# K as one tile of 64 KB rows in an attention decode kernel, with both products first and wo loaded near the end

## The chip, the cores and the metric

One core of a Trainium2 chip. The time is the device time of one execution in us. The experiments e1 to e4, e7, e10 and e11 ran on one chip and e5, e6, e8 and e9 on another, each beside the kernel before on the same chip (medians of 658.7 to 658.9 on both). A ratio below is the mean time of one kernel's fast runs over that of the other's of the same rounds, with a 95% interval; it is not quite the ratio of the medians that stand beside it.

## The reference, cut to what matters

One decode step for two rows: layernorm, attention over a cache of 8192 positions with 32 heads of 128, output projection, a second layernorm and a small ReLU-gated FFN.

```python
q = (layernorm(x) @ wq)                                  # 2 x 32 heads x 128
scores = einsum("bhqd,bhkd->bhqk", q, k_cache) / sqrt(128)
o = einsum("bhqk,bhkd->bhqd", softmax(scores), v_cache)  # k_cache, v_cache: 2 x 32 x 8192 x 128 bf16
h = x + o @ wo
h2 = h + ffn(layernorm(h))
```

The two caches are 268 of the 281 MB that are read, each byte used once.

## The kernel before

The work is cut into 16 passes of 4 heads. A pass has 8.4 MB of K and 8.4 MB of V. K comes in two halves of 4.2 MB into two buffers (rows of 32 KB), V in one tile (rows of 64 KB) into one buffer. For each half of K, DVE multiplies 96 of 128 positions of a row with q and folds the products by additions; TensorE transposes the other 32 and multiplies them with q; ACT takes the exps. When both halves have their exps, TensorE multiplies them with V (64 matmuls).

```python
K = [sb(f"K{i}", [128, SLOT], BF16) for i in range(2)]     # 32 KB a row each
V = sb("V", [128, 2 * SLOT], BF16)                         # 64 KB a row
...
# DVE, loop over passes
for q in range(PG):                                        # the two halves
    if q == 0:
        nc.vector.wait_ge(g2d, 1)
    nc.vector.wait_ge(k_sem[q], 16)
    nc.vector.sem_inc(k2p, 1)                              # TensorE may start
    run_d(k_mult(q))                                       # product
    last_d()
    nc.vector.sem_inc(d2s, 1)                              # K half free (for DVE)
    k_adds(q, run_d, last_d)                               # four folding additions
    if q == 0:
        nc.vector.wait_ge(p2d, 1)
        normalize(Ob, run_d, last_d)
        ...
    run_d(k_reduce(q))
    last_d()
    nc.vector.sem_inc(d2a, 1)                              # ACT: exps of DVE's part
...
# SP, pass by pass (p counts halves)
if p + 2 < NP:
    sp.wait((d2s, p + 1), tokp("kf", p))                   # product done, transposes done
    load_k(p + 2)
if p % 2 == 1 and p < P0 - 3:
    sp.wait(tokp("pv", p))                                 # all 64 products with V done
    load_v(p // 2 + 1, 0, 2 * J, v_sem[0])
```

The softmax here doesn't subtract the row's maximum and nothing guards it: scores larger than these inputs give would overflow.

## Time and profile before

| | |
|---|---|
| time before, beside the changed kernel | 659.11 us median of 6 (658.75 to 659.39) |
| one period (a K pair and a V tile, 16.78 MB) | 38.77 us |
| DVE busy in it | 28.80 us |
| V's load issued ahead of the leading DMA engine's turn | 10.3 to 11.9 us in the steady periods |

The timeline of the kernel before, SyncE's issues alone (start, length, line, what is loaded; the first line merges two issues, of K's first half at 312.34 and of its second at 327.75):

```profile
312.34 15.74 SPq L186 DMA_DIRECT2D K<-in_A_k_cache_dram  x2
341.20 0.33 SPq L189 DMA_DIRECT2D V<-in_A_v_cache_dram  x1
```

(The single transfer records don't name the engine. In the stream 16 packets are under way at a time, and nearly all start within 6 ns of the end of another; by that I put them in 16 rows below, and every tile then has 8 of its 128 packets in each row, in the order of issue.)

### The profile page before, as it was taken

The page shows a single profiled execution, that of the slowest core. Times are in us where ns is not written, and L with a number is a line of the kernel's source. Part 1 is how long each engine was busy: PE and PEld are TensorE (multiplying, and loading weights), DVE is VectorE, ACT ScalarE, POOL GpSimd, SP SyncE. Part 2 cuts the span into 40 slices and gives each one's busy share as a digit, 9 for nine tenths or more (in the row PEclk, how much of TensorE's full clock was granted, in tenths as well). Part 3 has the DMA queues.
Part 4 walks back from the last instruction along what each step waited for, and adds up shares of the span by engine and source line. Part 5 has one row for each costly group of instructions (what it writes and reads, how often), then busy time and mean ns, then how long its engine had stood idle before and what let it go on. Part 6 is the DMA issues. An engine that isn't in the chain of part 4 may idle for free.

```text
span 657.5 us, 7820 instructions
## 1 busy us (share of the span) xinstructions
PE 306.7 (47%) x3096; PEld 202.9 (31%) x3097; DVE 469.1 (71%) x275; ACT 274.0 (42%) x687; POOL 25.5 (4%) x96
## 2 busy tenths in 40 slices
PE   2644345444354445436444443644445354445466
PEld 0331232323233232323314232331323233133234
DVE  1594594958949496794949769494985949589881
ACT  1642343433454254344424534442454435335271
POOL 4000000000000000000000000000000000002000
PEclk9856557655575755557565575756557575556676
DMA  9999999999999999999999999999999999999997
GB/s 383 422 437 430 437 439 419 470 391 447 425 462 433 403 447 415 470 397 439 445 419 458 403 447 417 443 441 423 443 419 462 405 437 447 417 429 433 429 421 310
DMA packets 8629, 281.17 MB, mean 428 GB/s; under 512 B 966, under 2 KB 1068, under 8 KB 1580
## 3 DMA queue, kind: packets, MB, share of 16 engines
q1 hardware_dynamic: 8612, 281.06, 99.3%
q8 instruction: 5, 0.08, 0.1%
q14 instruction: 4, 0.03, 0.0%
q10 hardware_dynamic: 8, 0.00, 0.0%
HBM read 281.05 MB, written 0.00 MB: 427 GB/s over the span
## 4 chain that ended last, share of the span: by engine, by line
DMA 80%; DVE 15%; PE 3%; issue 1%; ACT 0%; DVEq 0%; SPq 0%
DMA K<-in_A_k_cache_dram 69%; DVE prod L563 15%; DMA V<-in_A_v_cache_dram 5%; DMA K<-in_B_W_gate_dram 4%; DMA V<-in_A_wq_dram 2%; PE T L345 1%; PE O L428 1%; PE O L272 1%; ACT kT L589 0%; PE O L775 0%; PE O L827 0%; PE O L330 0%; PE Ob L440 0%; PE T L405 0%; DVE prod L281 0%
## 5 line engine op out<-in xcount | busy, mean ns | idle before, releaser
L563 DVE TENSOR_TENSOR prod<-K,q_c 128x12288 bf16<-128x12288 bf16 x32 | 209.9, 6558 | 146.7 <-DMA K<-in_A_k_cache_dram 136.0
L572 DVE TENSOR_TENSOR prod<-prod 128x6144 bf16<-128x6144 bf16 (+3 forms) x128 | 212.2, 1658 | 7.8
L405 PE MATMUL T<-ident_f,K 128*128 128x128 f32 x512 | 123.3, 403 | 134.6 <-DVEq L611 134.6
L589 ACT ACTIVATE kT<-T 128x1024 bf16<-128x1024 bf16 x128 | 127.1, 1022 | 122.7 <-PE T L405 118.7
L428 PE MATMUL O<-V,e 128*16 128x512 bf16 x1024 | 91.4, 533 | 111.8 <-DMA V<-in_A_v_cache_dram 111.8
L517 ACT ACTIVATE e<-scores 32x96 bf16<-32x96 f32 x128 | 53.9, 421 | 196.5 <-DVEq L625 193.3
L405 PEld LDWEIGHTS T<-ident_f,K 128*128 128x128 f32 x512 | 88.6, 206 | 137.6 <-DVEq L611 137.5
L428 PEld LDWEIGHTS O<-V,e 128*16 128x16 bf16 x1024 | 30.5, 117 | 165.3 <-DMA V<-in_A_v_cache_dram 113.3
L388 PE MATMUL S<-q_c,kT 128*128 128x8 bf16 x1024 | 48.6, 171 | 44.8 <-ACT kT L589 44.6
L388 PEld LDWEIGHTS S<-q_c,kT 128*128 128x128 bf16 x1024 | 41.9, 107 | 73.1 <-ACT kT L589 71.3
L440 PE MATMUL Ob<-sel,os_sb 128*128 128x4 f32 x136 | 30.2, 345 | 38.4 <-ACT os_sb L592 38.4
L440 PEld LDWEIGHTS Ob<-sel,os_sb 128*128 128x128 f32 x136 | 28.7, 312 | 40.3 <-ACT os_sb L592 40.2
L517 ACT ACTIVATE e<-S 32x32 bf16<-32x32 f32 x128 | 29.8, 233 | 16.1 <-PE S L388 15.0
L577 DVE TENSOR_REDUCE scores<-prod 128x96 f32<-128x768 bf16 x32 | 30.5, 953 | 2.8
L517 ACT ACTIVATION_READ_ACCUMULATOR e<-scores 32x1 f32 x128 | 30.0, 235 | 0.0
L517 ACT ACTIVATION_READ_ACCUMULATOR e<-S 32x1 f32 x128 | 25.6, 200 | 1.5
L589 ACT ACT_TABLE_LOAD x15 | 19.2, 1283 | 0.3
L560 POOL COPY q_c<-q_all 128x144 bf16<-128x144 bf16 x16 | 7.5, 472 | 243.5 <-PE O L428 231.3
L592 ACT ACTIVATE os_sb<-O 128x512 f32<-128x512 f32 x17 | 10.1, 597 | 15.3 <-PE O L428 14.9
L544 POOL MEMSET O_l<- 128x32 bf16 x13 | 1.7, 130 | 299.8 <-DVEq L622 299.8
L281 DVE CAST prod<-O 128x512 bf16<-128x512 f32 x1 | 0.7, 692 | 11.0 <-PE O L272 11.0
L272 PE MATMUL O<-V,xlT 128*2 128x512 bf16 x32 | 3.4, 600 | 7.7 <-DMA V<-in_A_wq_dram 7.7
(103 smaller groups left out, 94.2 us busy)
## 6 DMA issues: line engine op xcount, KB each, us to landing
K<-in_A_k_cache_dram SPq DMA_DIRECT2D x32, 4096.0 KB, 29.2
V<-in_A_v_cache_dram SPq DMA_DIRECT2D x3, 4096.0 KB, 31.7
V<-in_A_wq_dram SPq DMA_DIRECT2D x1, 4096.0 KB, 12.3
X<-in_A_wo_dram SPq DMA_DIRECT2D x1, 3584.0 KB, 46.2
V<-in_A_v_cache_dram SPq DMA_DIRECT2D x1, 3072.0 KB, 23.1
K<-in_B_W_up_dram SPq DMA_DIRECT2D x1, 1376.0 KB, 23.6
K<-in_B_W_gate_dram SPq DMA_DIRECT2D x1, 1376.0 KB, 26.6
V<-in_A_v_cache_dram SPq DMA_DIRECT2D x1, 1024.0 KB, 25.2
```

Source lines behind the costliest of these rows:

```text
L272: mm = nc.tensor.matmul(Op[i][32 * t:32 * t + B, :], lhsT=lT[:, c * B:(c + 1) * B], rhs=wq[:, c, n:n + 512], start=(c == 0), stop=(c == DC ...
L388: i = nc.tensor.matmul(Sp[p % 2][:, A * jj:A * jj + 2 * A], lhsT=kv_[:, k, r, :], rhs=q_c[:, 2 * A * r:2 * A * r + 2 * A], start=(r == 0), ...
L405: i = nc.tensor.transpose(Tp[g % 2][:, k * 128:(k + 1) * 128], k_t[:, j:j + 2, :].rearrange("p j d -> p (j d)").bitcast(F32), ident_f[:])
L428: i = nc.tensor.matmul(Op[0][c:c + 16, :], lhsT=e_t[q][:, j // VJ, :], rhs=v_t[:, j:j + VJ, :].rearrange("p j d -> p (j d)"), start=(q == ...
L440: i = nc.tensor.matmul(Ob[:, 0:A], lhsT=os_sb[:, jj * Dh:(jj + 1) * Dh], rhs=sel[:, A * jj:A * jj + A], start=(jj == 0), stop=(jj == VJ - 1))
L517: i = nc.scalar.activation(out=e_t[q][h, j0 // VJ:j1 // VJ, :].rearrange("p g (j a) -> p g j a", a=A)[:, :, :, a], in_=src(h, a), func=ACT ...
L560: nc.gpsimd.tensor_copy(out=q_c[:], in_=q_all[:, o]).then_inc(g2d, 1)
L563: return nc.vector.tensor_tensor(out=prod[:, 0:JC, :], in0=tile(K[p % 2], p)[:, 0:JC, :], in1=q_c[:, Q2:QW].unsqueeze(1).broadcast_to([128 ...
L572: run(nc.vector.tensor_tensor(out=prod[:, 0:JC, 0:w], in0=prod[:, 0:JC, 0:w], in1=prod[:, 0:JC, w:2 * w], op=ALU.add))
L577: return nc.vector.tensor_reduce(out=scores[p % PG][:, 0:JC], in_=prod[:, 0:JC, 0:8], axis=AX.X, op=ALU.add)
L589: to_pe(nc.scalar.activation(out=kT[gg % 2][:], in_=Tp[gg % 2][:].bitcast(BF16), func=ACT.Copy))
L592: to_pe(nc.scalar.activation(out=os_sb[:], in_=Op[0][:], func=ACT.Copy))
```

## The change

Intent: K gets the packets of 64 KB that V has. The room for it: K becomes one buffer of 64 KB rows, so the next K can only load once both halves of this one have been read. Hence DVE makes both products first, into two scratch tiles (wo's tile X serves as the second, so wo loads near the end), and TensorE takes both halves in a row, with the sums and exps on ACT behind.

```diff
-        K = [sb(f"K{i}", [128, SLOT], BF16) for i in range(2)]
+        K = sb("K", [128, 2 * SLOT], BF16)
+        prods = [X[:, 0:JC * Dh].rearrange("p (j d) -> p j d", d=Dh), prod]
 ... TensorE, loop
                     k_part(body, 0, (1, 2, 3, 4), ((k2p, 1),))
-                    collect(body, 6)
-                    k_part(body, 1, (8, 9, 10, 11), ((k2p, 2),))
-                    pv(body, 0, ((JC, J, ((v_sem[0], 16),)), (0, JC, ())))
-                    pv(body, 1, ((JC, J, ((v_sem[1], 16), (a2p, 12))), (0, JC, ((a2p, EV),))))
+                    k_part(body, 1, (5, 6, 7, 8), ())
+                    collect(body, 9)
+                    pv(body, 0, ((JC, J, ((v_sem, 16), (a2p, 10))), (0, JC, ((a2p, 12),))))
+                    pv(body, 1, ((JC, J, ()), (0, JC, ((a2p, EV),))))
 ... DVE, loop
-                    for q in range(PG):
-                        ... wait, k_mult(q), k_adds(q), (normalize), k_reduce(q)
+                    for q in range(PG):
+                        run_d(k_mult(q, prods[q]))
+                    last_d()
+                    nc.vector.sem_inc(d2s, 1)
+                    for q in range(PG):
+                        k_adds(prods[q], run_d, last_d)
+                        if q == 0:
+                            nc.vector.wait_ge(p2d, 1)
+                        run_d(k_reduce(q, prods[q]))
+                        last_d()
+                        nc.vector.sem_inc(d2a, 1)
+                        if q == 0:
+                            nc.vector.sem_inc(d2s, 1)
+                            normalize(Ob, run_d, last_d)
 ... ACT, loop: all 8 evictions, then sums(), both exp_pe, both exp_dve
 ... SP
-                    if p + 2 < NP:
-                        sp.wait((d2s, p + 1), tokp("kf", p))
-                        load_k(p + 2)
+                    if p % 2 == 1 and p < P1:
+                        o = p // 2 + 1
+                        sp.wait((d2s, 2 * o - 1), tokp("kf", p))
+                        if o < NI:
+                            load(K, A_k_cache, o, k_sem[0])
+                            sp.wait(tokp("pv", p))
+                            load(V, A_v_cache, o, v_sem)
+                        else:
+                            ... half of K, wo into X, the other half, V in three pieces
```

More of the change, by code (lines that the diff above doesn't have):

```diff
@@ L95, in bass_sequential_preLN__gqa_block_cached__glu_gated_reglu__decode_kernel @@
         k_sem = [S(f"k{i}") for i in range(2)]
-        v_sem = [S(f"v{i}") for i in range(2)]
+        v_sem = S("v")
         a2p, k2p, l2p = S("a2p"), S("k2p"), S("l2p")
@@ L167, in bass_sequential_preLN__gqa_block_cached__glu_gated_reglu__decode_kernel, with kv_rows, load @@
         ZC = 64
-        def k_rows(p):
-            hq, b = divmod(p // 2, B)
-            return A_k_cache[b, A * hq:A * hq + A].rearrange(
-                "h (p k j) d -> k (h p) (j d)", p=128 // A, k=2)[p % 2]
-        def v_rows(o):
+        def kv_rows(cache, o):
             hq, b = divmod(o, B)
-            return A_v_cache[b, A * hq:A * hq + A].rearrange("h (p j) d -> (h p) (j d)", p=128 // A)
+            return cache[b, A * hq:A * hq + A].rearrange("h (p j) d -> (h p) (j d)", p=128 // A)
         def tile(x, p):
-            return x[:].rearrange("p (k j d) -> p k j d", j=J, d=Dh)[:, p % 2 if x is V else 0]
+            return x[:].rearrange("p (k j d) -> p k j d", j=J, d=Dh)[:, p % 2]
         if True:
             def program():
-                def load_k(p):
-                    nc.sync.dma_start(K[p % 2][:], k_rows(p)).then_inc(k_sem[p % 2], 16)
-                def load_v(o, k0, k1, sem):
-                    nc.sync.dma_start(V[:, k0 * Dh:k1 * Dh], v_rows(o)[:, k0 * Dh:k1 * Dh]).then_inc(sem, 16)
+                def load(x, cache, o, sem, k0=0, k1=2 * J):
+                    nc.sync.dma_start(
+                        x[:, k0 * Dh:k1 * Dh], kv_rows(cache, o)[:, k0 * Dh:k1 * Dh]).then_inc(sem, 16)
                 nc.scalar.dma_start(x_row, A_x[:, 0]).then_inc(sem_x, 16)
@@ L194, in program @@
                     wo_rows, A_wo[128 * DR:].rearrange("(p r) n -> p (r n)", r=4)).then_inc(sem_wl, 16)
-                load_k(0)
-                load_k(1)
+                load(K, A_k_cache, 0, k_sem[0])
                 pool.run(nc.gpsimd.memset(ident_f[:], 0.0))
@@ L317, in program @@
                 sp.wait(t_q)
-                load_v(0, 0, 2 * J, v_sem[0])
-                nc.sync.dma_start(
-                    X[:], A_wo[0:128 * DR].rearrange("(p r) n -> p (r n)", r=DR)).then_inc(sem_wo, 16)
+                load(V, A_v_cache, 0, v_sem)
                 t_mm, t_cp = {}, {}
@@ L361, in program @@
                                  start=True, stop=True)
-                nc.tensor.sem_inc(v_sem[1], 16 * (NI - 1))
                 EV = 13
@@ L373, in mark @@
                         self.at[key] = pe.run(inst)[1] - self.base
-                body = Tokens(pe.count)
+                body, tail = Tokens(pe.count), Tokens(0)
                 def k_part(T, p, ev, k_wait):
-                    k_t = tile(K[p % 2], p)
+                    k_t = tile(K, p)
                     wait = nc.tensor.wait_ge
@@ L390, in score @@
                                     rhs=q_c[:, 2 * A * r:2 * A * r + 2 * A], start=(r == 0), stop=(r == 1))
-                                if loop and g == NG - 2 and k == r == 0:
+                                if loop and p % 2 and g == NG - 2 and k == r == 0:
                                     T.mark(("kf", p), i)
@@ L434, in pv @@
                             n += 1
-                    T.mark(("pv", p), i)
+                    if T is tail or q:
+                        T.mark(("pv", p), i)
                 def collect(T, a):
@@ L469, in program @@
                     nc.tensor.sem_inc(l2p, -1)
-                    for sem in v_sem:
-                        nc.tensor.sem_inc(sem, -16)
-                    nc.tensor.sem_inc(k2p, -2)
+                    nc.tensor.sem_inc(v_sem, -16)
+                    nc.tensor.sem_inc(k2p, -1)
                     nc.tensor.sem_inc(a2p, -EV)
@@ L475, in program @@
                 pe.count = body.base + NI * n_body
-                tail = Tokens(0)
                 P0, P1 = NP - 2, NP - 1
@@ L489, in program @@
                 tail.mark("op", i)
-                pv(tail, P0, ((JC, J, ((v_sem[0], 16),)), (0, JC, ((a2p, 13),))))
+                pv(tail, P0, ((JC, J, ((v_sem, 16),)), (0, JC, ((a2p, 13),))))
                 nc.tensor.wait_ge(a2p, 14)
@@ L558, in q_copy, with k_mult, k_adds @@
                     else:
-                        pool.wait(tokp("fp", 2 * o - 2), (d2s, 2 * o))
+                        pool.wait(tokp("fp", 2 * o - 2), (d2s, 2 * o - 1))
                     nc.gpsimd.tensor_copy(out=q_c[:], in_=q_all[:, o]).then_inc(g2d, 1)
-                def k_mult(p):
+                def k_mult(p, pr):
                     return nc.vector.tensor_tensor(
-                        out=prod[:, 0:JC, :], in0=tile(K[p % 2], p)[:, 0:JC, :],
+                        out=pr[:, 0:JC, :], in0=tile(K, p)[:, 0:JC, :],
                         in1=q_c[:, Q2:QW].unsqueeze(1).broadcast_to([128, JC, Dh]), op=ALU.mult)
-                def k_adds(p, run, last):
+                def k_adds(pr, run, last):
                     w = Dh
@@ L572, in k_adds, with k_reduce @@
                         run(nc.vector.tensor_tensor(
-                            out=prod[:, 0:JC, 0:w], in0=prod[:, 0:JC, 0:w], in1=prod[:, 0:JC, w:2 * w], op=ALU.add))
+                            out=pr[:, 0:JC, 0:w], in0=pr[:, 0:JC, 0:w], in1=pr[:, 0:JC, w:2 * w], op=ALU.add))
                     last()
-                def k_reduce(p):
+                def k_reduce(p, pr):
                     return nc.vector.tensor_reduce(
-                        out=scores[p % PG][:, 0:JC], in_=prod[:, 0:JC, 0:8], axis=AX.X, op=ALU.add)
+                        out=scores[p % PG][:, 0:JC], in_=pr[:, 0:JC, 0:8], axis=AX.X, op=ALU.add)
                 def exp_pe(p):
@@ L605, in last_d @@
                             nc.vector.wait_ge(d2d, n_d[0])
+                    nc.vector.wait_ge(g2d, 1)
+                    nc.vector.wait_ge(k_sem[0], 16)
+                    nc.vector.sem_inc(k2p, 1)
                     for q in range(PG):
-                        if q == 0:
-                            nc.vector.wait_ge(g2d, 1)
-                        nc.vector.wait_ge(k_sem[q], 16)
-                        nc.vector.sem_inc(k2p, 1)
-                        last_d()
-                        run_d(k_mult(q))
-                        last_d()
-                        nc.vector.sem_inc(d2s, 1)
-                        k_adds(q, run_d, last_d)
+                        run_d(k_mult(q, prods[q]))
[3 more added lines that the diff above has]
+                        k_adds(prods[q], run_d, last_d)
                         if q == 0:
                             nc.vector.wait_ge(p2d, 1)
+                        run_d(k_reduce(q, prods[q]))
[3 more added lines that the diff above has]
+                            nc.vector.sem_inc(d2s, 1)
                             normalize(Ob, run_d, last_d)
@@ L622, in program @@
                             nc.vector.sem_inc(d2g, 1)
-                        run_d(k_reduce(q))
-                        last_d()
-                        nc.vector.sem_inc(d2a, 1)
-                    for sem, n in ((d2d, n_d[0]), (g2d, 1), (p2d, 1), (k_sem[0], 16), (k_sem[1], 16)):
+                    for sem, n in ((d2d, n_d[0]), (g2d, 1), (p2d, 1), (k_sem[0], 16)):
                         nc.vector.sem_inc(sem, -n)
@@ L630, in program @@
                 with nc.Fori(0, NI, engines=OrderedEngineSet([nc.scalar.engine])):
-                    n_a = 0
+                    n_a = (NG + 1) * PG
                     for q in range(PG):
                         for gg in range(NG):
-                            n_a += 1
-                            nc.scalar.wait_ge(p2a, n_a)
+                            nc.scalar.wait_ge(p2a, (NG + 1) * q + gg + 1)
                             evac(gg)
-                        n_a += 1
-                        nc.scalar.wait_ge(p2a, n_a)
+                    nc.scalar.wait_ge(p2a, n_a)
+                    sums()
+                    for q in range(PG):
                         exp_pe(q)
-                        if q == 0:
-                            sums()
+                    for q in range(PG):
                         nc.scalar.wait_ge(d2a, q + 1)
@@ L660, in program @@
                         dve.last()
-                        t_dm[p] = dve.run(k_mult(p))
-                        k_adds(p, dve.run, dve.last)
+                        t_dm[p] = dve.run(k_mult(p, prod))
+                        k_adds(prod, dve.run, dve.last)
                         if p == P0:
-                            dve.wait(tokp("pv", p - 2))
-                        t_s[p] = dve.run(k_reduce(p))
+                            dve.wait(tokp("pv", p - 1))
+                        t_s[p] = dve.run(k_reduce(p, prod))
                         if p == P0:
@@ L697, in program @@
                         exp_dve(p)
-                    if p + 2 < NP:
-                        sp.wait((d2s, p + 1), tokp("kf", p))
-                        load_k(p + 2)
-                    if p % 2 == 1 and p < P0 - 3:
-                        sp.wait(tokp("pv", p))
-                        load_v(p // 2 + 1, 0, 2 * J, v_sem[0])
-                    elif p == P0 - 3:
-                        sp.wait(tokp("pv", p))
-                        load_v(NI - 1, 0, J, v_sem[0])
-                    elif p == P0 - 2:
-                        load_v(NI - 1, J, 2 * J, v_sem[1])
-                    elif p == P0 - 1:
-                        sp.wait(tokp("pv", p - 1))
-                        load_v(NI, 0, J, v_sem[0])
-                        sp.wait(tokp("pv", p))
-                        for k, (j0, j1) in enumerate(((V_LAST, J), (0, V_LAST))):
-                            load_v(NI, J + j0, J + j1, sem_vl[k])
+                    if p % 2 == 1 and p < P1:
[6 more added lines that the diff above has]
+                        else:
+                            load(K, A_k_cache, o, k_sem[0], 0, J)
+                            sp.wait((d2s, 2 * o))
+                            nc.sync.dma_start(
+                                X[:], A_wo[0:128 * DR].rearrange("(p r) n -> p (r n)", r=DR)).then_inc(sem_wo, 16)
+                            load(K, A_k_cache, o, k_sem[1], J, 2 * J)
+                            sp.wait(tokp("pv", p))
+                            load(V, A_v_cache, o, v_sem, 0, J)
+                            for k, (j0, j1) in enumerate(((V_LAST, J), (0, V_LAST))):
+                                load(V, A_v_cache, o, sem_vl[k], J + j0, J + j1)
                     if p == NP - 2:
@@ L719, in program @@
                             nc.sync.dma_start(
-                                K[0][:, k * DC * F:(k + 1) * DC * F],
+                                K[:, k * DC * F:(k + 1) * DC * F],
                                 w.rearrange("(p c) n -> p (c n)", c=DC)).then_inc(sem_w[k], 16)
@@ L723, in program @@
                             nc.sync.dma_start(
-                                K[0][:, 2 * DC * F + r0 * D:2 * DC * F + (r0 + n) * D],
+                                K[:, 2 * DC * F + r0 * D:2 * DC * F + (r0 + n) * D],
                                 B_W_down[r0 * 128:(r0 + n) * 128].rearrange("(p r) n -> p (r n)", r=n)).then_inc(sem_wd[k], 16)
@@ L758, in program @@
                     in1=Sp[0][:, 0:B].unsqueeze(1).broadcast_to([128, DC, B]), op=ALU.subtract))
-                wup, wgt = (K[0][:, k * DC * F:(k + 1) * DC * F].rearrange("p (c f) -> p c f", c=DC)
+                wup, wgt = (K[:, k * DC * F:(k + 1) * DC * F].rearrange("p (c f) -> p c f", c=DC)
                             for k in range(2))
-                wdn = K[0][:, 2 * DC * F:2 * DC * F + 10 * D].rearrange("p (r n) -> p r n", n=D)
+                wdn = K[:, 2 * DC * F:2 * DC * F + 10 * D].rearrange("p (r n) -> p r n", n=D)
                 pe.wait(t_d)
```

## The prediction

> **What bounds the kernel now.** I began with the page of the kernel before: its slices, its queues, its chain.
>
> ```profile
> DVE  1594594958949496794949769494985949589881
> ...
> DMA  9999999999999999999999999999999999999997
> ...
> DMA packets 8629, 281.17 MB, mean 428 GB/s; under 512 B 966, under 2 KB 1068, under 8 KB 1580
> ...
> q1 hardware_dynamic: 8612, 281.06, 99.3%
> ...
> DMA 80%; DVE 15%; PE 3%; issue 1%; ACT 0%; DVEq 0%; SPq 0%
> ```
>
> See that the DMA row is at 9 in every slice but the last, and that one queue fills 99.3% of the 16 engines' span; DVE, the busiest compute engine, swings between 1 and 9 and always has idle slices. The chain gives DVE 15%, but that is a product that releases a K load, followed by a wait of 32 us until that load lands. So I asked whether the stream ever ran dry, with the busy times of three periods of the loop (a period is one pair of K halves and one V tile, 16.78 MB):
>
> ```profile
> 305.61:344.40 38.79, 18.53 (x174) 12.03 (x174) 28.80 (x15) 16.75 (x42) 1.02 (x5) 0.55 1.00 433
> 344.40:383.17 38.77, 18.49 (x174) 12.50 (x174) 28.80 (x15) 16.70 (x42) 1.02 (x5) 0.57 1.00 432
> 383.17:421.94 38.77, 17.02 (x174) 11.65 (x174) 28.80 (x15) 16.69 (x42) 1.03 (x5) 0.60 1.00 433
> ```
>
> The columns after the length are PE, PEld, DVE, ACT and POOL busy us, the clock, the DMA share and GB/s. DMA share is 1.00 in each; DVE needs 28.80 of 38.77 us. The single transfer records of the trace confirm it: from 1.8 us to 654.8 us no moment is without a transfer. The time is the stream's length plus about 2 us ahead and 3 us behind. A change can win only by making the stream's packets cheaper, and lose only by leaving it empty.
>
> [...] this core alone reads at 433.[...] tiles land in the order of issue (K at 305.6, V at 334.6), and SP shows the waits. [...] the order of the loads (wo early or late) costs nothing by itself. [...] the product takes 6557 to 6560 ns in all 32 cases, and nothing in the change alters its shape or type.
>
> **The change part by part.**
>
> *Packets.* A row of a K half is one packet of 32 KB, a row of V one of 64 KB. From the transfer records between the first K packet and the first V packet of steady periods: a K pair holds the leading engine 19.426 us (16 packets), a V tile 19.350 us (8 packets): 0.076 us per 8.39 MB. The change turns 15 K pairs, and V's tile 14 that went as two halves, into 64 KB rows: 16 x 0.076 = 1.2 us. The last K tile stays in halves. wo is the same 3.67 MB elsewhere.
>
> *The new period.* K has now one buffer of 64 KB rows, as V has. Call t the moment when K of a pass lands. V of the pass lands at t+19.35 and K of the next would at t+38.70. The durations come from one period of before:
>
> ```profile
> 305.69 6.56 DVE L563 TENSOR_TENSOR prod<-K,q_c 128x12288 bf16<-128x12288 bf16 x1 [8.93 <-DMA K<-in_A_k_cache_dram]
> ...
> 312.34 15.74 SPq L186 DMA_DIRECT2D K<-in_A_k_cache_dram  x2
> ...
> 312.40 6.73 DVE L572 TENSOR_TENSOR prod<-prod 128x6144 bf16<-128x6144 bf16 x4
> 319.17 0.18 DVE L525 TENSOR_REDUCE zr<-Ob 128x4 f32<-128x16 f32 x1
> ...
> 319.90 0.95 DVE L577 TENSOR_REDUCE scores<-prod 128x96 f32<-128x768 bf16 x1
> ```
>
> These are whole lines of the timeline: start, length, engine, instruction. The first is the product, then the issue of two K loads 0.1 us behind it, the four folding additions, the start of the normalisation (0.7 us in all with gaps) and the last reduction.
>
> K's release: the landing at 305.61 is 0.08 before the product. Two products, 2 x 6.56 + 0.1, end at t+13.3. TensorE's part of one half took 5.8 us (305.66 to the last score at 311.4), and two in a row have no exp between their evictions: the last transpose is read by t+11. So the products release K at t+13.3. From issue to first packet I have one measurement, the first load: issued at 0.81, first packet 1.85, so 1.0 us. Next K is ready at t+14.4. The 16 engines are not in step: the leading one ends a tile 2.1 us before the last, and the landing comes 0.5 us after the last one's end. V's packets end at t+16.7 (leading engine) to t+18.8 (last). Slack 2.3 to 4.4 us: the stream stays fed.
>
> V's release is the tighter one, for V cannot be freed before the scores of both halves are exps. DVE: additions and reduction of half 0 after t+13.3, 6.8 + 1.0 = t+21.1; normalisation, t+21.9; half 1, another 7.8 = t+29.7. ACT: the exps of the DVE part of one half took 1.75 us (320.94 to 322.7): t+31.6. TensorE then has only the last 24 of 64 products with V left; the 64 took 6.46 us at 334.69, so 24 take 2.5: t+34.2. SP issues next V at once (before: PE ended at 341.15, SP issued at 341.20), first packets t+35.3. K's packets end at t+36.1 (leading) to t+38.2 (last): slack 0.8 to 2.9 us. An engine that leads and runs dry for less than its lead of 2 us costs nothing, because the landing waits for the last. So I expect no loss from the single K buffer, though DVE now does all its additions in front of V's release.
>
> *Start.* The first K tile lands where the second K half did, near 35.3 us; DVE's first product moves from 26.4 to there. That is 9 us of compute later, and nothing in the stream: V's first tile is issued at 16.6 as before, the next K at 35.3 + 13.3 = 48.7 while the first V runs until 52.2 (leading engine).
>
> *End.* After tile 14 of V: half of K (released at t+13.3), wo (scratch X is free once half 0 is reduced, t+21.1; half of K runs until t+28), the other half, V's last tile in three pieces, the FFN weights. Each is issued 5 us or more before its turn. The last K half stands as far from the stream's end as before, so the tail behind it, which ends in the wait for W_gate (651.77 in the chain) and 5.7 us after it, stays.
>
> *Sum.* 659.2 - 1.2 = 658.0 us.
>
> **Rivals.** (1) V's release comes later than its slack: any excess beyond 2.9 us costs its full size in 14 or 15 periods. If DVE or TensorE needed 4 us more in the chain above, 15 x 1.1 = 17 us, 675 us. For it: the chain of two sets of additions, exps and 24 products has just 0.8 us against the leading engine. Against: DVE's durations vary by 3 ns in 32 cases, and the granted clock of 0.55 to 0.60 already holds for the PE times that I used. (2) K's single buffer leaves the stream idle for the two products, 13.3 us a period, 186 us in all: it would be so if V's 19.35 us were not queued between, but they are. (3) DVE or the chain's 15% shrink and the time falls by some per cent: against it the DMA share of 1.00; a shorter compute chain has nothing to give, as DVE already waits 8.9 us for K in each period. (4) No gain at all, if packets of 64 KB for K do not run as V's do: 659.2.
>
> **Range and chances.** The packet gain could be 0 to 1.8 us (from packet medians of 1218 and 2422 ns: 16 x 8 x 14 ns = 1.8); a slight starvation of some periods could give 1 or 2 us back. Range 656.9 to 659.8. A gain over 2% would need 13 us out of a stream with no gap: 1%. A loss over 2% needs rival 1: 4%. Within 2%: 95%.
>
> **What would show it.** Right: DMA share 1.00 in periods of 38.70 us; the K load issued 13.3 us after a landing, V's load some 34 us after it; 16 x 128 = 2048 fewer packets (8629 to near 6581); DVE idle 9 us a period, all at the loop's top. Wrong: a period over 38.8 us, a DMA share below 1.00 just before V's or K's first packets, SP waiting for the products with V until after t+36, or DVE products on X slower than 6.56 us.

Three sentences are conclusions of mine that had no run behind them then. That a change can lose only by leaving the stream empty was concluded from the records without a gap (1.8 to 654.8 us); slow first packets, below, turned out to be another way. That an engine which runs dry for less than its lead costs nothing is an estimate, from the 2.1 us by which the leading engine ended a tile before the last. That wo's place costs nothing was measured only afterwards, in e6 (ratio 0.9999).

## More of the kernel before

V's load is issued at 341.2. By the single transfer records the leading engine ended the K pair before it at 351.55: ten microseconds in hand.

## The result, and the profile after

659.26 us, median of 6 runs (658.6 to 660.3), against 659.11 (658.75 to 659.39): ratio 1.0004, interval 0.9992 to 1.0017. The 1.2 us that I had expected to gain are not there, and the runs scatter over 1.7 us in place of 0.6. The profile came from the fastest of the six runs (658.6), which is to be kept in mind. Its page:

```profile
DMA  9999999999999999999999999999999999999997
...
DMA packets 6324, 281.16 MB, mean 428 GB/s; under 512 B 710, under 2 KB 812, under 8 KB 1324
...
q1 hardware_dynamic: 6308, 281.05, 99.2%
...
DMA 65%; DVE 32%; PE 2%; issue 1%; ACT 0%; SPq 0%; DVEq 0%; ACTq 0%
```

The packets are as predicted: 2048 fewer of data, and 256 fewer records of 4 bytes (16 for each of 16 loads that are gone). The queue is full as before. DVE's share of the chain doubled, because two products now stand in front of each K load, and the time is the same: a share in that chain (15%, then 32%) was no cost here, with the queue at 99.2% of the span. Busy times of two late periods (length, then PE, PEld, DVE, ACT, POOL, clock, DMA share, GB/s):

```profile
344.98:383.66 38.68, 20.13 (x174) 12.51 (x174) 28.71 (x15) 16.53 (x42) 6.21 (x5) 0.50 1.00 434
383.66:422.37 38.71, 17.80 (x174) 10.44 (x174) 28.71 (x15) 16.30 (x42) 6.21 (x5) 0.63 1.00 433
```

38.70 us a period as predicted, 0.07 less than before. One pass on the timeline, DVE first, then SP:

```profile
306.36 6.56 DVE L552 TENSOR_TENSOR X<-K,q_c 128x12288 bf16<-128x12288 bf16 x1 [9.12 <-DMA K<-in_A_k_cache_dram]
312.83 6.55 DVE L552 TENSOR_TENSOR prod<-K,q_c 128x12288 bf16<-128x12288 bf16 x1
319.53 6.73 DVE L561 TENSOR_TENSOR X<-X 128x6144 bf16<-128x6144 bf16 x4
326.30 0.95 DVE L566 TENSOR_REDUCE scores<-X 128x96 f32<-128x768 bf16 x1
...
328.23 6.73 DVE L561 TENSOR_TENSOR prod<-prod 128x6144 bf16<-128x6144 bf16 x4
334.99 0.95 DVE L566 TENSOR_REDUCE scores<-prod 128x96 f32<-128x768 bf16 x1
```

```profile
319.47 0.33 SPq L182 DMA_DIRECT2D K<-in_A_k_cache_dram  x1
340.57 0.33 SPq L182 DMA_DIRECT2D V<-in_A_v_cache_dram  x1
```

K landed at 306.27 (0.09 before the product). Its successor is issued 13.2 us later (predicted 13.3), V's 34.3 us later (predicted 34.2). So the chain of releases was worked out right, and late periods run at the predicted length. The loss is in the early ones. The chain of waits shows when each K tile is taken up:

```profile
35.15 6.56 DVE X L552
...
73.74 6.56 DVE X L552
...
112.84 6.56 DVE X L552
...
151.54 6.56 DVE X L552
```

The distances are 38.59, 39.10 and 38.70: 0.4 us went in the second, and the transfer records show where. V's second tile was issued at 69.38, and the leading engine ended K at 71.41, 2.0 us later. With the 1.0 us that I had allowed for from issue to first packet, that is ample. But 14 of the 16 engines took 2.5 to 3.8 us over their first packet of that tile, in place of 2.42, and three of the 16 had stood idle first. The records don't name them; paired in the order that fits an early finisher with the latest start, the idle times are 0.6, 0.8 and 1.9 us, and in any pairing the latest of the three, which started at 73.29, had stood idle for 1.6 us or more: it had finished K among the first ten and used up its whole lead. Two engines started at that moment, the late one and the one that had ended K last; the records don't tell them apart. One took 2.49 us over its packet, the other 2.85, 0.4 us too long, and so set the landing: that is the 0.4 us. In all, 33 of the 224 first packets of V's tiles 1 to 14 took over 2.5 us.

A second thing may hide a gain of this size in single traces. At the end of V's next to last piece the last engine was 1.09 us ahead of the kernel before (641.10 against 642.19); at the end of W_gate only 0.33 us (650.95 against 651.28). In between, an instruction fetch of 16 KB (queue 8 of the page) took 1.07 us, in the place of one engine's packets. Whether that engine was the one that ended W_gate last the records don't say. The next to last ended it at 650.20, 0.76 us earlier, so the fetch could account for all of the loss of 0.76, and is not shown to.

So there are two theories. **Theory 1**: V's load now comes too late for a clean start, and slow first packets eat the gain, more in some runs. **Theory 2**: the gain is there in each run, and only fetches that fall on the last engine hide it. A third, that larger packets are worth nothing, is already unlikely by the 38.70 us.

### The profile page after: what moved, and what is told of

It is laid out like the page before. It is cut to its first block, busy times and chain, and to the rows that moved or that the text cites. A ratio compares the mean times of both kernels' runs of the same rounds, so it can differ in the third digit from the quotient of the medians.

```text
span 657.3 us, 7744 instructions
## 1 busy us (share of the span) xinstructions
PE 337.1 (51%) x3097; PEld 207.1 (32%) x3097; DVE 467.8 (71%) x275; ACT 271.2 (41%) x687; POOL 95.3 (15%) x96
## 3 DMA queue, kind: packets, MB, share of 16 engines
q1 hardware_dynamic: 6308, 281.05, 99.2%
## 4 chain that ended last, share of the span: by engine, by line
DMA 65%; DVE 32%; PE 2%; issue 1%; ACT 0%; SPq 0%; DVEq 0%; ACTq 0%
DMA K<-in_A_k_cache_dram 59%; DVE X L552 15%; DVE prod L552 15%; DMA K<-in_B_W_down_dram 5%; DVE prod L561 1%; DVE X L561 1%; PE T L395 0%; PE O L418 0%; DVE scores L566 0%; PE Ob L431 0%; ACT e L506 0%; PE O L816 0%; ACT kT L578 0%; SPq L708 0%; PE S L378 0%
## 5 line engine op out<-in xcount | busy, mean ns | idle before, releaser
L418 PE MATMUL O<-V,e 128*16 128x512 bf16 x1024 | 114.7, 612 | 187.6 <-ACT e L506 113.0
L552 DVE TENSOR_TENSOR X<-K,q_c 128x12288 bf16<-128x12288 bf16 x15 | 98.4, 6558 | 141.8 <-DMA K<-in_A_k_cache_dram 141.8
L395 PE MATMUL T<-ident_f,K 128*128 128x128 f32 x512 | 126.0, 410 | 65.3 <-DVEq L598 60.8
L561 DVE TENSOR_TENSOR prod<-prod 128x6144 bf16<-128x6144 bf16 (+1 forms) x68 | 112.7, 1658 | 4.0
L552 DVE TENSOR_TENSOR prod<-K,q_c 128x12288 bf16<-128x12288 bf16 x17 | 111.4, 6553 | 2.9 <-DMA K<-in_A_k_cache_dram 2.1
L395 PEld LDWEIGHTS T<-ident_f,K 128*128 128x128 f32 x512 | 91.5, 211 | 67.4 <-DVEq L598 62.8
L561 DVE TENSOR_TENSOR X<-X 128x6144 bf16<-128x6144 bf16 (+3 forms) x60 | 99.5, 1658 | 3.8
L378 PE MATMUL S<-q_c,kT 128*128 128x8 bf16 x1024 | 48.7, 171 | 35.1 <-ACT kT L578 34.9
L538 POOL COPY rsel<-rows 128x112 bf16<-128x112 bf16 x14 | 44.1, 3151 | 41.2 <-DVEq L615 40.4
L506 ACT ACTIVATE e<-S 32x32 bf16<-32x32 f32 x128 | 29.7, 232 | 2.4 <-PE S L378 0.9
L540 POOL TENSOR_TENSOR O_l<-O_cur,mask 128x32 bf16<-128x32 bf16 x14 | 25.0, 1785 | 0.0
L549 POOL COPY q_c<-q_all 128x144 bf16<-128x144 bf16 x16 | 16.2, 1010 | 45.3 <-PE O L418 32.3
## 6 DMA issues: line engine op xcount, KB each, us to landing
V<-in_A_v_cache_dram SPq DMA_DIRECT2D x1, 3072.0 KB, 29.7
```

The source lines that it names most:

```text
L378: i = nc.tensor.matmul(Sp[p % 2][:, A * jj:A * jj + 2 * A], lhsT=kv_[:, k, r, :], rhs=q_c[:, 2 * A * r:2 * A * r + 2 * A], start=(r == 0), ...
L395: i = nc.tensor.transpose(Tp[g % 2][:, k * 128:(k + 1) * 128], k_t[:, j:j + 2, :].rearrange("p j d -> p (j d)").bitcast(F32), ident_f[:])
L418: i = nc.tensor.matmul(Op[0][c:c + 16, :], lhsT=e_t[q][:, j // VJ, :], rhs=v_t[:, j:j + VJ, :].rearrange("p j d -> p (j d)"), start=(q == ...
L506: i = nc.scalar.activation(out=e_t[q][h, j0 // VJ:j1 // VJ, :].rearrange("p g (j a) -> p g j a", a=A)[:, :, :, a], in_=src(h, a), func=ACT ...
L538: e.tensor_copy(out=rsel[:, :, o % B, :], in_=bass.AP(x.tensor, x.offset, [list(x.ap[0]), [DR - OS, A], [1, DR]]))
L540: e.tensor_tensor(out=w, in0=O_cur[:].unsqueeze(2).broadcast_to([128, A, NM]), in1=mask[:, off // 4:off // 4 + OS // 4 * (A - 1) + 1:OS // ...
```

## The experiments

### The changed kernel again, and DVE's part made shorter

e1_again has no edit.

> The changed kernel once more, unaltered, for its spread and a second profile. Theory 1 (V's release has no slack: the load reaches the engines 2 us or more after its issue, leading engines run dry, and how much of the packets' 1.2 us that eats differs from run to run): median 659.0 to 659.6, runs spread over 1 us or more, slow first packets of V tiles in the new profile too, V issued 34.3 us after each landing of K. Theory 2 (the gain of 1.2 us is there in every run, and only instruction fetches of 1 us that fall on the last engine hide it): the V tiles start without gaps in the new profile, and the spread is like that of the kernel before (0.6 us).

Measured: 659.91 us (659.22 to 660.58, 5 runs), ratio to before 1.0013 (0.9999 to 1.0027). That is 0.3 us above the median that Theory 1 gave; the spread, 1.4 us, is as it said, and 53 of 224 first V packets took over 2.5 us.

e2_less_dve gives TensorE five groups of 8 positions of a row in place of four, so DVE has 88 in place of 96 (`JC = J - NG * GT`); the rest of the edit adjusts the counts of the semaphores.

```diff
-    NG = 4
+    NG = 5
...
-                    k_part(body, 0, (1, 2, 3, 4), ((k2p, 1),))
-                    k_part(body, 1, (5, 6, 7, 8), ())
-                    collect(body, 9)
-                    pv(body, 0, ((JC, J, ((v_sem, 16), (a2p, 10))), (0, JC, ((a2p, 12),))))
+                    k_part(body, 0, (1, 2, 3, 4, 5), ((k2p, 1),))
+                    k_part(body, 1, (6, 7, 8, 9, 10), ())
+                    collect(body, 11)
+                    pv(body, 0, ((JC, J, ((v_sem, 16), (a2p, 12))), (0, JC, ((a2p, 14),))))
```

> Five groups of 8 rows on TensorE in place of four, DVE's part 88 rows in place of 96: DVE's chain in front of V's release shrinks by a twelfth of 29.6 us, 2.5 us. Theory 1: V is issued about 31.8 us after the landing, no slow first packets, median 658.0, ratio to before 0.998, spread as of the kernel before. Theory 2: V is issued earlier too, but time and spread are those of e1_again, 659.2.

Measured: 657.68 us (657.54 to 657.79), ratio 0.9981 (0.9968 to 0.9995). The whole predicted gain is there, and the spread is 0.25 us. The timelines of both, the first product of each pass and what ended the idle time before it; e1_again first:

```profile
74.38 6.56 DVE L552 TENSOR_TENSOR X<-K,q_c 128x12288 bf16<-128x12288 bf16 x1 [9.24 <-DMA K<-in_A_k_cache_dram]
113.39 6.56 DVE L552 TENSOR_TENSOR X<-K,q_c 128x12288 bf16<-128x12288 bf16 x1 [9.43 <-DMA K<-in_A_k_cache_dram]
152.18 6.56 DVE L552 TENSOR_TENSOR X<-K,q_c 128x12288 bf16<-128x12288 bf16 x1 [9.20 <-DMA K<-in_A_k_cache_dram]
191.44 6.56 DVE L552 TENSOR_TENSOR X<-K,q_c 128x12288 bf16<-128x12288 bf16 x1 [9.67 <-DMA K<-in_A_k_cache_dram]
```

and e2_less_dve:

```profile
74.14 6.02 DVE L552 TENSOR_TENSOR X<-K,q_c 128x11264 bf16<-128x11264 bf16 x1 [11.30 <-DMA K<-in_A_k_cache_dram]
112.85 6.03 DVE L552 TENSOR_TENSOR X<-K,q_c 128x11264 bf16<-128x11264 bf16 x1 [11.32 <-DMA K<-in_A_k_cache_dram]
151.55 6.02 DVE L552 TENSOR_TENSOR X<-K,q_c 128x11264 bf16<-128x11264 bf16 x1 [11.31 <-DMA K<-in_A_k_cache_dram]
190.25 6.03 DVE L552 TENSOR_TENSOR X<-K,q_c 128x11264 bf16<-128x11264 bf16 x1 [11.31 <-DMA K<-in_A_k_cache_dram]
```

Periods of 39.01, 38.79 and 39.26 us against 38.71, 38.70 and 38.70. That DVE works 0.54 us less in a product is not the reason: it waits for K in both kernels, longer in e2 (11.3 us against 9.2 to 9.7). What moved is the issue of V's second tile, at 69.77 in e1_again and 67.38 in e2_less_dve:

```profile
69.77 0.33 SPq L182 DMA_DIRECT2D V<-in_A_v_cache_dram  x1
```

```profile
67.38 0.33 SPq L182 DMA_DIRECT2D V<-in_A_v_cache_dram  x1
87.57 0.33 SPq L182 DMA_DIRECT2D K<-in_A_k_cache_dram  x1
106.07 0.33 SPq L182 DMA_DIRECT2D V<-in_A_v_cache_dram  x1
```

None of the 224 first packets of V took over 2.5 us. Theory 2 expected no gain; it is out as the explanation. The time of the fetch doesn't separate the kernels either: it lies at 638.8 to 638.9 in e2 and also in both of the next two runs, of which one has the gain and one has not.

### The lead taken back

e2 also changes TensorE's and ACT's work. To tell the lead from these, e10 and e11 keep the five groups and hold V's release back by repeating the last reduction of a pass once or twice (a repeat writes the same values).

```diff
-                        run_d(k_reduce(q, prods[q]))
-                        last_d()
+                        for _ in range(1 + 2 * q):      # e11; 1 + 1 * q in e10
+                            run_d(k_reduce(q, prods[q]))
+                            last_d()
```

> e2_less_dve with the last reduction of each pass three times, which gives back nearly the whole lead that the shorter DVE part had won: V's load is issued some 2.3 us ahead of the leading engine's turn, near the 2.0 us of the changed kernel, in place of 4.1 us. If the lead of that load is the cause, the gain is gone: 658.5 to 659.5, spread up, slow first V packets. If something else in the five groups is the cause (clock, other order), it stays at 657.6.

> The same with the last reduction twice: lead about 3.2 us. First packets started 2.5 us and more after the issue were mostly clean in the changed kernel, so 657.5 to 658.2; if 3.8 us are needed (the shortest lead that I saw always clean), 658.3 to 659.

Measured: e11 658.6 us (657.88 to 659.38), ratio 0.9997 (0.9984 to 1.0011); e10 657.44 us (657.33 to 657.62), ratio 0.9979 (0.9966 to 0.9993). V's second tile was issued at 68.80 in e11 and at 68.00 in e10:

```profile
68.80 0.33 SPq L182 DMA_DIRECT2D V<-in_A_v_cache_dram  x1
```

```profile
68.00 0.33 SPq L182 DMA_DIRECT2D V<-in_A_v_cache_dram  x1
```

The gain goes when the lead goes, and stays while a lead of 3.4 us stays. All runs of this kind in one table; the lead is the time from the issue of V's load to the end of K's tile on the leading engine, by the records, over V's tiles 1 to 14 of the profiled run:

| kernel | lead, us | first V packets over 2.5 us, of 224 | median, us | spread of its runs, us |
|---|---|---|---|---|
| e1_again | 1.7 to 2.8 | 53 | 659.91 | 1.4 |
| changed kernel | 2.0 to 2.5 | 33 | 659.26 | 1.7 |
| e11_less_dve_late2 | 2.6 to 2.7 | 15 | 658.60 | 1.5 |
| e10_less_dve_late1 | 3.35 to 3.4 | 0 | 657.44 | 0.3 |
| e2_less_dve | 3.9 to 4.1 | 0 | 657.68 | 0.25 |
| e9 (e2 again) | 4.1 to 4.3 | 0 | 657.43 | 0.2 |

The three kernels whose lead is over 3.3 us have no slow starts, and less time and scatter than the three with a lead under 2.9; within each three the order is not strict. Between 2.8 us (the largest lead with a slow start, one packet of 2.54 us in e1_again) and 3.35 us lies the point from which all starts of V's tiles were clean. Below it the lead alone does not decide: in the changed kernel V's tiles 11 to 14, with leads of 2.44 to 2.47 us, started clean, while tile 2, with 2.48, had slow packets. K's loads in the same trace are a second check: their lead is 3.8 to 4.3 us, and none of their 224 first packets (tiles 1 to 14) took over 2.5 us. It is no sharp point either: in e9 two K loads with leads of 3.2 and 3.4 us had six between them, of 2.5 to 3.0 us, and the gain held. What the DMA hardware does in that time the traces don't show.

e9 repeated e2 on another chip, and its gain held: ratio 0.9979 (0.9966 to 0.9993).

> e2_less_dve unaltered, beside the next one on the same chip, to repeat its gain. Theory 1: 657.5 to 658.0 us, ratio 0.998 again, V's packets in all 15 tiles at 2.42 us from the first. If e2's gain was luck of that chip: 658.9 to 659.3, ratio near 1.000.

### The packets alone

e3 and e8 load K in two parts of 32 KB rows again, released and awaited together; e3 from the changed kernel, e8 from e2.

```diff
-                            load(K, A_k_cache, o, k_sem[0])
+                            load(K, A_k_cache, o, k_sem[0], 0, J)
+                            load(K, A_k_cache, o, k_sem[0], J, 2 * J)
...
-                    nc.vector.wait_ge(k_sem[0], 16)
+                    nc.vector.wait_ge(k_sem[0], 32)
```

> Only K's loads are cut in two of 32 KB rows again, released and awaited together. If K's larger packets are worth 15 x 0.076 us, this is 1.1 us slower than e1_again (about 660.4; K tiles take 19.43 us of an engine in place of 19.35). If they are worth nothing in time, equal to e1_again.

> e9 with K's loads cut in two of 32 KB rows. Where nothing runs dry, the packets alone should show: 15 x 0.076 = 1.1 us slower than e9, so 658.8, the time of the kernel before. e3 showed only 0.65 us, and I take the rest for the extra 0.07 us of lead that V's load then has in each period; if that is wrong, e8 is 0.65 us slower than e9.

Measured: e3 660.56 us (660.2 to 661.19), 0.65 over e1_again of the same rounds. e8 659.30 us (659.08 to 659.35), 1.87 over e9. In the profiles a K tile of e8 takes 19.43 us of an engine and one of e9 19.35; at the end of V's next to last piece e8 is 1.32 us behind, of which 15 x 0.08 = 1.2 are K's packets; the profiled spans differ by 1.4 us (657.6, 656.2), and so do the medians of all their runs (657.5, 656.1). The other 0.5 us lie behind the last instruction: in each run of e3 and e8 the time is 1.7 to 1.9 us longer than the core's span, in each run of every other kernel here 1.2 to 1.4 us. Only the traces of these two show an instruction fetch of 8 KB there, about 1 us after the span's end (at 658.62 in e8, 660.08 in e3); that it is the cause was not tested. So on clean starts the packets are worth 1.2 to 1.4 us, near the 1.1 us expected. By spans e3 shows only 0.2 us of it (medians 658.8 and 658.6). The lead of V in its profile was 1.9 to 2.2 us, with some 30 slow first packets in place of 53 in e1_again; whether that is the rest stays open, as the scatter of e1 and e3 (1.4 and 1.0 us) is larger than what is missing. e8 is also a control: five groups with the old packets are no faster than the kernel before (ratio 1.0007).

### wo's place

e6 is the kernel before with wo's load moved behind the first of the last two K halves.

```diff
                 load_v(0, 0, 2 * J, v_sem[0])
-                nc.sync.dma_start(X[:], A_wo[0:128 * DR]...).then_inc(sem_wo, 16)
...
                     elif p == P0 - 2:
+                        nc.sync.dma_start(X[:], A_wo[0:128 * DR]...).then_inc(sem_wo, 16)
                         load_v(NI - 1, J, 2 * J, v_sem[1])
```

> The kernel before with only wo's load moved from the start to behind the first of the last two K halves. Theory: the stream is full either way, so 658.6 to 659.3, ratio 0.999 to 1.001. Rival: the late wo costs in the tail, up to 1 us, 660.

Measured: 658.78 us (658.56 to 659.03), before 658.74, ratio 0.9999 (0.9986 to 1.0013). The place of wo costs nothing.

### V's release held back in the changed kernel

e4 and e5 repeat the last reduction in the changed kernel once and three times.

```diff
-                        run_d(k_reduce(q, prods[q]))
-                        last_d()
+                        for _ in range(1 + 3 * q):      # e5; 1 + 1 * q in e4
+                            run_d(k_reduce(q, prods[q]))
+                            last_d()
```

> The last reduction of each pass is done twice, which holds V's release back by 1.0 us (issue at 35.3 us after the landing). Theory 1: the slack of the last engine is nearly used up, 660 to 668 us, slow or late first packets in most V tiles. The prediction's slack of 2.9 us for the last engine: 659.2, no change.

> The last reduction four times, which holds V's release back by 3.0 us (issue 37.3 us after the landing, when the leading engine is 1 us dry). Theory 1, from e4 where 1.0 us cost 0.5 us a period: each further us should cost its full size in each of 15 periods, so 6.7 + 2 x 15 = 37 us over, 690 to 698. If only single unlucky packets cost something: below 675.

Measured: e4 666.62 us (664.79 to 667.39), ratio 1.0121; e5 670.22 us (668.95 to 676.86), ratio 1.0174. e4 shows that no slack was left: one microsecond of work on an engine with 9 us of idle time a period cost 7. In its profile V's lead was 0.8 to 2.3 us, and some 140 of 224 first packets took over 2.5 us. e5 missed my expectation by 20 us and fell where its other branch had it, below 675. I had carried e4's slope on, as though a late load cost its full delay. It does not: 1.0 us of delay had already cost about 7, and three times as much cost 11. In e5's profile V is issued 37.3 us after the landing (72.22 against 34.94), and its first packets follow 1.0 us later, at 38.2, just when the last engine ends K (38.2 by the prediction's own figure). In this tile the loss lies in the first packets: 14 of them took 2.7 to 3.4 us, the other two started later. In all, the page's queue line (97.7% of 675.5 us, against 99.2% of 657.3 in the changed kernel) puts some 8 us of this run's extra 18 down to longer packets and some 10 to engines without a packet, as a mean over the 16. The longest of the first four periods, 41.78 us, shows both on one engine. Its V load is issued at 150.55, and the last engine ends K at 152.34; 15 engines start V by then, one only at 153.71, after 1.4 us or more without work, and it takes 3.88 us over its first packet: 1.4 + 1.5 = 2.9 of the 3.1 us by which the period exceeds 38.70. Why that engine started late the traces don't show:

```profile
35.03 6.56 DVE X L552
...
73.88 6.56 DVE X L552
...
113.36 6.56 DVE X L552
...
152.73 6.56 DVE X L552
...
194.51 6.56 DVE X L552
```

(These periods of the chain of e5's profiled run, the slowest of its five, are 38.85, 39.48, 39.37 and 41.78 us.) What is shown is that lateness can cost from 2.7 us of lead downwards, and not in step with the delay.

### The order on DVE

e7 has DVE in the old order in the changed kernel: the second product only behind the first half's additions.

```diff
                     for q in range(PG):
                         run_d(k_mult(q, prods[q]))
-                    last_d()
-                    nc.vector.sem_inc(d2s, 1)
-                    for q in range(PG):
+                        last_d()
+                        if q == 1:
+                            nc.vector.sem_inc(d2s, 2)
                         k_adds(prods[q], run_d, last_d)
```

> DVE in the order of the kernel before (product, additions, reduction, then the second product), all else as changed: K is released some 22 us after its landing in place of 13.3, first packets at 23, where the last engine ends V at 18.8. The stream should stand idle 4 us and lose some 0.5 us to slow first packets in each of 15 periods: 715 to 735 us. If the order of the products does not matter for the single buffer: 659.

Measured: 756.09 us (754.88 to 756.94), ratio 1.1476. The page's queue line and busy times of two periods:

```profile
q1 hardware_dynamic: 6308, 281.05, 87.5%
```

```profile
343.00:433.00 90.00, 39.90 (x348) 25.35 (x348) 57.69 (x30) 33.01 (x84) 20.35 (x10) 0.52 0.87 373
```

The stream is empty 13% of the time. The mechanism is as expected, the size was 20 to 40 us too low. K is issued 23.4 us after its landing, not 22, because the first reduction now waits 1.5 us for TensorE:

```profile
365.02 0.95 DVE L566 TENSOR_REDUCE scores<-X 128x96 f32<-128x768 bf16 x1 [1.46 <-PE Ob L431]
...
373.49 0.33 SPq L182 DMA_DIRECT2D K<-in_A_k_cache_dram  x1
```

and from there to the landing at 395.35 pass 21.9 us, where 1.0 + 19.35 + 0.5 = 20.9 had been counted. I put the other 1.0 us down to slow first packets; that is an estimate, for they were not counted in this run. 23.4 + 21.9 = 45.3 us a period. With one buffer for K, both products had to come first here.

## Why the prediction was right or wrong

- **The stream bounds the kernel, and DVE's share of the chain is no cost.** Right: a DVE share of 32% in place of 15% left the time as it was, and a shorter DVE part (e2) paid only through the load that it let go.
- **Packets, 1.2 us.** Right: periods of 38.70 us where starts are clean, and 1.2 us of K packets between e8 and e9 by the profile (1.4 us in their spans; 1.87 us in their times, with 0.5 us behind the last instruction). e2 shows the predicted time: I had said 658.0, e2 and e9 ran at 657.68 and 657.43.
- **K's release at 13.3 us, V's at 34.2 us.** Right: 13.2 and 34.3. A detail of the sum for V is loose: its own terms, 29.7 + 1.75 + 2.4, make 33.9, and 34.2 was written. The reading of the shown lines that two K loads are issued 0.1 us behind the product is also wrong: the line merges two issues, and the second is at 327.75, behind the second product; nothing in the sum rests on it.
- **V's slack.** This step failed. It read: "first packets t+35.3. K's packets end at t+36.1 (leading) to t+38.2 (last): slack 0.8 to 2.9 us. An engine that leads and runs dry for less than its lead of 2 us costs nothing". Its last sentence was an estimate. I took the 1.0 us from the first load of the kernel, which found idle engines, as all that a load needs, and counted only idle time as loss. The runs show that of loads issued 2.0 to 2.7 us ahead some started with slow packets (33 of 224 over 2.5 us in the changed kernel, 15 in e11), also on the engines that came last, and that 3.35 us were enough (none in e10). Nor was a load free to wait while earlier ones were still queued: with 2.0 to 2.7 us of queued work left, it did cost. The release was right to 0.1 us; the term that was mis-sized is the latency behind it.
- **Start and end.** Right: wo's place costs nothing (e6), and the second K load went out at 48.26 (48.7 predicted). Only "5 us or more before its turn" was too much for the half of K behind V's tile 14, which was issued 4.2 us ahead (590.37 against 594.59).
- **Rivals.** The first, a late V release, is what happened, in a mild form: no period lost its excess in full. The range had allowed for "a slight starvation of some periods" of 1 or 2 us, but the text expected none, and not by slow packets. The fourth, no gain from the packets, has the number (659.2) but not the cause, by the periods of 38.70 us and by e8. The second, a stream idle during the products, is what e7 shows when their order is undone.
- **The time.** 659.26 lies in the range, nearer to its upper end than to 658.0, and the forecast of "within 2%" held. The 1.2 us of gain and about as much of slow starts cancelled.

## What to carry to other kernels

Where a stream of loads is the bound, look for every load at its lead: the time from its issue until the DMA engines reach it, not only whether the queue ran dry. Going from two buffers to one spent that lead here (V's lead of 10.3 us and more became 2.0 to 2.5, as more work came to stand in front of its release), so count how many microseconds are left and whether a little work can be moved off the chain that releases the buffer; here a twelfth of DVE's part turned no gain into the full one. A DMA share of 1.00 and an unchanged engine did not show a loss of 0.2%: scatter between runs was its first sign.

## Other figures of these runs

- From the start of an issue to its first packet it took 0.96 us at the shortest (e5, on idle engines), of which the issuing instruction itself took 0.33 us; the first load of the kernel took 1.04 us (issued at 0.81, first packet at 1.85, in the kernel before). In the full stream, loads issued 1.7 to 2.8 us ahead had 15 to 53 of 224 first packets of 64 KB at 2.5 to 3.9 us in place of 2.42; at 3.35 us and more none of V's were (six of K's were in e9, at 3.2 and 3.4 us).
- The one core of these runs read at 433 to 434 GB/s in a steady period of the changed kernel, at 432 to 433 in the kernel before.
- 8.39 MB took an engine 19.43 us in rows of 32 KB and 19.35 in rows of 64 KB.
- Instruction fetches of 16 KB, five a run in the kernel before and in the changed one, took 0.98 to 1.14 us each. The one of 1.07 us in the changed kernel lies ahead of the end of W_gate, where the last engine ended 0.76 us after the next.
- A copy of 128x112 elements on GpSimd took 0.28 us in the kernel before, where it ran beside the reduction on DVE, and 3.15 us in the changed one, where it ran beside an addition. Why was not tested; it costs no time here, as POOL is busy for 6.21 of 38.7 us in a period. The two timelines, before and after:

```profile
320.24 0.28 POOL L549 COPY rsel<-rows 128x112 bf16<-128x112 bf16 x1
```

```profile
405.96 3.15 POOL L538 COPY rsel<-rows 128x112 bf16<-128x112 bf16 x1
```
